# Transposes of half batch 12 and the first expert's weight rests moved behind the first list's one-hots; the logits of the last half batches in single groups

## The chip, the cores and the metric

The kernel runs on one core of a Trainium2 chip. The metric is the time of the whole program on the device, in microseconds (us), as the median of several executions. TensorE (PE) does the matrix products, VectorE (DVE) and ScalarE (ACT) the elementwise work, GpSimd (POOL) issues the indirect DMAs and did some subtractions, SyncE (SP) issues most other DMAs. Each engine works through its own queue strictly in the order in which the program was written for it, and waits there for results of others.

## The reference

```python
# 1. a causal 7-tap filter for each of 8 heads (weights: softmax over the taps)
out = np.einsum('hk,bskhg->bshg', w, x_unf)          # x: (8, 3584, 192)
# 2. a mixture of 8 experts with room for N/E = 3584 tokens each
x = out.reshape(28672, 192)
flat = (x @ w_gate).flatten()
for idx in np.argsort(-flat):                        # best (token, expert) pair first
    tok, e = idx // E, idx % E
    if assigned[tok] >= 0 or counts[e] >= cap: continue
    assigned[tok] = e; counts[e] += 1
for e in range(E):
    mask = assigned == e
    out[mask] = np.maximum(x[mask] @ w1[e], 0) @ w2[e]   # 192 -> 1024 -> 192
```

## The kernel before, in words

**Stages.** The 28672 tokens are 16 half batches of 1792. Stage one, up to some 160 us, runs over the half batches `i`: `load` brings `X`, `conv` makes eight products (`cv`, one for each head `h`), ACT copies each to the tile `a`, and a DMA stores `a` to `attn`. For the gate, DVE transposes `a` in four steps (`transp(i, u)`, tile `aT`), PE makes six groups of logits from it (`gates`, or `gate(i, u)` for two groups of it; into `pl`, copied to `L`), and `end(i)` transposes them (`pt`), copies them to `LT` (ACT) and takes the best logit of each token (`top`, DVE, tile `M1`). Stage two, the FFN, runs over 56 tiles of 512 tokens, expert by expert: POOL gathers the tokens (`xg`), PE transposes them, ACT and DVE split each number into a high and a low part (`xa`, `xd`), then for each of eight `f`: five products into `ph`, ACT takes the relu (`hh`), DVE the rest (`hl`), and PE multiplies with `w2` into `y`, one tile later.

**The lists.** Which tokens go to which expert is found in between. A first list needs only the first eight half batches: `sort` builds 16 one-hot tiles `oa` on DVE (`TENSOR_TENSOR oa<-irep,q`), PE multiplies with them (`bg<-X,oa`), ACT copies the sums; then `turn` (16 transposes `bg<-identb,X`, copied by ACT to `X`), `gather` (17 products, copied to `asm`) and `tokens` (16 small DVE operations that end in the index lists `ia`, `ja`). The first two tiles are gathered by `ja`; `todo` holds the transposes and splits of tile 0. A second and a third list follow during the FFN (`half(1)`, `rest`); there `sort4` sends its sums through DRAM (`otab`).

**What sets the order.** One Python program writes all queues. A conv step `(i, h)` calls `mid(h)` after its product and before ACT's copy of it; what `mid` writes there stands at that place in every engine's queue. The list steps are generators (`Steps`) that a hook advances when a model of the engines' times (`Pace`: `nc.pe`, `nc.dve`, `nc.act`) says that their inputs are ready. During tile 0 of the FFN the calls counted in `TAIL` advance the generator `tail` (the last logits). `wsplit` splits one piece of an expert's weights: ACT copies the high part (`w<-raw`), the engine given as an argument takes the rest (`w<-raw,w` or `dl<-raw,w`), and the raw buffer's next DMA is issued.

Where it stood before: from half batch 13 on (`LAG`), transposes and logits wait in the list `left` until the first list is written (`got`); the first four pieces of expert 0 are split at `(14, 1)`, `(14, 3)`, `(14, 5)` and `(14, 7)` with POOL as the engine; the logits of half batches 14 and 15 stand in `tail`.

Of the kernel before, what the change touches and what calls it, by code (L numbers as in the profile page):

```python
# [18 lines left out]
PEW, PEA = "pe", "pe after act"  # L19
# [9 lines left out]
class Meter:  # L29


    def __init__(self, pace, name, eng):
        self.pace, self.name, self.eng = pace, name, eng
# [226 lines left out]
class Route:  # L260
# [4 lines left out]
    def __init__(self, tc, nc, LT, cst, wk, drm):  # L265
        self.tc, self.nc, self.LT, self.cst, self.wk = tc, nc, LT, cst, wk
        self.cols = 0
        self.M1 = cst.tile([128, G], F32, name="M1")
        self.Ts = cst.tile([128, 1], F32, name="Ts")
        self.bad = cst.tile([128, 1], F32, name="bad")  # L270
        self.identr = cst.tile([128, 128], FR, name="ident")
        self.ident = self.identr.bitcast(F32)
        self.ltab = drm.tile([128, 8, G], F32, name="ltab")
        self.otab = [drm.tile([128, 16, 128], BF, name="otab%d" % q) for q in range(2)]
# [200 lines left out]
    def sort(self, h, nt, base, per=8):  # L475

        nc, wk = self.nc, self.wk
        V, A, PE = nc.vector, nc.scalar, nc.tensor
        O = self.O = wk.tile([128, 128, 16], BF, name="X1")
        q = []  # L480
        g0 = z = 0
        free = [0.0, 0.0]
        while z < 128:

            t = max(q[0][1] + nc.las, free[0] if z % 32 == 0 else 0.0) if q else 0.0
            if q and t <= nc.pe:
                if z == 64:
                    yield from self.columns(h, nt, base)
                a = q.pop(0)[0]
                if z % 32 == 0:  # L490
                    ps = self.bg()
                for u in range(per):
                    c = 16 * (z % 32 + u)
                    PE.matmul(ps[:, c:c + 16], a[:, :, u], self.b[:, :, :, z + u], start=True, stop=True,
                              skip_group_check=True)
                if z % 32 == 32 - per:
                    A.activation(O[:, z - 32 + per:z + per].rearrange("p g w -> p (g w)"), ps, AF.Copy)
                    free = [free[1], nc.act + nc.las]
                z += per
            elif g0 < 128 and len(q) < 5:  # L500
                a = self.oh_pool.tile([128, 128, per], BF, name="oa")
                V.tensor_tensor(a, self.irep[:, :, 0:per], self.q[:, None, g0:g0 + per].to_broadcast([128, 128, per]),
                                op=OP.is_equal)
                q.append((a, nc.dve))
                g0 += per
            else:

                yield t
                nc.pe = max(nc.pe, t)
                continue  # L510
            yield
        yield PEA
# [963 lines left out]
PERIOD, START = 8.8, 11.0  # L1476
LAG = 13

TAIL = (2, 3, 4, 7, 8, 9, 12, 13)


def moe_kernel(ctx, tc, x, weight, wg, w1, w2, out):
    nc = Pace(tc.nc)
    V, P = nc.vector, nc.gpsimd
# [4 lines left out]
    with ExitStack() as cw:  # L1489
# [8 lines left out]
        r = Route(tc, nc, LT, lst, wk, drm)  # L1498
        r.oh_pool = oh
        r.bg = lambda: bgp.tile([128, 512], F32, name="bg")  # L1500
        ff = FFN(tc, nc, attn, w1, w2, out, r.ident, wr, drm)
# [39 lines left out]

        def tail():

            for i in (14, 15):
                for u in range(3):
                    gate(i, u)
                    yield PEA if u == 2 else None
                end(i)
            nc.sync.dma_start(r.ltab, LT)
            c1.close()  # L1550
            cs.close()
            ff.wpool2(cw, 1)
            ff.hp[1] = pool(cw, "fh1", 1, **late)
            yield

        bg = Steps(nc, r, (half(0), tail(), half(1), rest()))
        bg.keep = 3
        cs, c1, ca, cl, cc = (ExitStack() for _ in range(5))
# [4 lines left out]
        k = build(cs, tc, nc, x, weight, wg, attn, LT, wk)  # L1563
# [15 lines left out]
        def end(i):  # L1579

            k.logits_t(i)
            r.top(i)

        def first():
            for e in range(2):
                ff.gather(e, [ja0[:, e, b:b + 1] for b in range(4)], NTOK // 2, P)


        todo = [partial(f, 0, *a) for u in range(2) for f, a in ((lambda i, u: ff.transp(i, u, r.bg()), (u,)), (ff.evac, (u,)))]
        got, left = [], []  # L1590

        def gate(i, u):
            for f in range(2 * u, 2 * u + 2):
                k.logits(i, f)

        def gates(i):
            for u in range(3):
                gate(i, u)

        def hook(at):  # L1600
            nc.pe = max(nc.pe, PERIOD * at / 8 + START)
            bg.hook(1.5)
            if not got and len(bg.gens) == 3:
                first()
                got.append(at)
            elif got and at >= got[0] + 10 and at % 8 in (2, 5) and todo:
                for _ in range(2):
                    todo.pop(0)()

        k.load(0)  # L1610
        k.toeplitz()
        k.gate_ops()
# [2 lines left out]
        for i in range(NHB):  # L1615
            if i + 3 < NHB:
                k.load(i + 3)
            if i == 4:
                r.consts_late()
            if i == 13:  # L1620
                cx[0].close()
                for _ in range(4):
                    ff.wload()
                ff.wpool(cw, 0, **late)

            def mid(h):

                if i and h == 0:
                    if i >= LAG:
                        left.append(partial(gates, i - 2))  # L1630
                    for u in range(4):
                        left.append(partial(k.transp, i - 1, u))
                        if 1 < i and (u == 3 or i < LAG):
                            left.append(partial(gate, i - 2, u) if u < 3 else partial(end, i - 2))
                for _ in range(2 if got else 1):
                    if left and (i < LAG or got):
                        left.pop(0)()
                if i >= 14 and h % 2:
                    ff.wsplit(-1, P)
                hook(8 * i + h)  # L1640

            k.conv(i, mid)
        for c in cx[1], cx[2], cx[3], cc:
            c.close()
        ff.pt = pool(cw, "pt", 1, space=PSUM, **right, **late)
# [3 lines left out]
        if not got:  # L1649
            first()  # L1650
        bg.keep = 0
        for f in left + todo:
            f()
        for u in range(4):
            k.transp(15, u)
# [25 lines left out]
        def steps():  # L1681
            if len(bg.gens) == 3:
                calls.append(0)
                if len(calls) in TAIL:
                    bg.run()
# [45 lines left out]
```

## Time and profile before

| what | value |
|---|---|
| median of 3 runs (lowest, highest) | 1240.46 us (1240.14, 1240.78) |
| the profiled execution, its own time | 1242.93 us |
| its span, first to last instruction | 1241.2 us |
| TensorE busy | 1202.9 us, 97% of the span |
| VectorE busy | 983.0 us, 79% |
| ScalarE, GpSimd busy | 565.0 and 537.8 us |
[...]

The profiled execution is 2.47 us longer than the median. The page shows TensorE busy in all but a few places, so what counts is where it is not: the waits of PE, and the chain of work that leads to each. Nearly all instructions carry line 56, the helper that records them, so operations are told apart by their tiles. A row of the chain shows only the time that the piece adds to the chain; a row in order of time shows the instruction's own duration, which overlaps its neighbours on a pipelined engine.

### The profile page before, as it was taken

What the parts mean: (1) busy time and instruction counts of PE and PEld (TensorE: products, weight loads), DVE (VectorE), ACT (ScalarE), POOL (GpSimd) and SP (SyncE); (2) the same over time, 40 slices, a digit from 0 to 9 for tenths busy, and PEclk for the clock granted to TensorE, in tenths of its full rate; (3) what the DMA queues carried; (4) which work ended last, traced back from release to release, by engine and by line L of the source; (5) the groups of instructions that cost most, each with busy time, mean ns of one, the idle gap of its engine ahead of it and who ended that gap; (6) DMA issues with size and microseconds to landing.
All of it is one profiled execution on the core that took longest, in us unless ns stands there. A gap on an engine that the chain in (4) does not pass through costs nothing.

```text
span 1241.2 us, 21781 instructions
## 1 busy us (share of the span) xinstructions
PE 1202.9 (97%) x7694; PEld 1036.0 (83%) x7694; DVE 983.0 (79%) x2117; ACT 565.0 (46%) x1252; POOL 537.8 (43%) x528
## 2 busy tenths in 40 slices
PE   4899999999999999999999999999999999999997
PEld 2445678899989989889888889999999999999997
DVE  7389689898998989989979865777777777777772
ACT  4454565556445455454554433343333333343332
POOL 3000254435556555555455435434534444543522
PEclk9999999999999999999999999999999999999999
DMA  9999774658527474756344342114223222413100
GB/s 212 331 348 320 234 244 120 155 170 287 174 76 213 135 241 124 223 158 193 89 131 120 108 106 73 41 41 158 90 104 105 100 98 96 155 64 131 48 23 29
DMA packets 129221, 182.03 MB, mean 147 GB/s; under 512 B 21632, under 2 KB 91728, under 8 KB 127440
## 3 DMA queue, kind: packets, MB, share of 16 engines
q1 hardware_dynamic: 86496, 104.15, 27.5%
q0 software_dynamic: 21504, 44.07, 11.9%
q10 hardware_dynamic: 21104, 32.34, 7.9%
q8 instruction: 62, 1.02, 0.4%
q14 instruction: 55, 0.45, 0.1%
HBM read 102.38 MB, written 78.12 MB: 145 GB/s over the span
## 4 chain that ended last, share of the span: by engine, by line
PE 89%; DVE 4%; DMA 4%; ACT 1%; issue 1%; SPq 0%; POOL 0%; ACTq 0%; POOLq 0%; DVEq 0%
PE ph L56 42%; PE y L56 40%; PE bg L56 3%; PE cv L56 3%; DMA X<-in_x_dram 2%; DVE aT L56 1%; DVE X L56 1%; PE pl L56 1%; DMA wgr<-in_moe_w_gate_dram 1%; PE px L56 0%; DMA otab<-X 0%; SPq L189 0%; DMA X<-otab 0%; ACT a L56 0%; ACT X L56 0%
## 5 line engine op out<-in xcount | busy, mean ns | idle before, releaser
L56 PE MATMUL y<-w,hh 128*128 128x384 f32 x1792 | 536.4, 355 | 0.0
L56 ACT ACTIVATE hh<-ph 128x512 fp32r<-128x512 f32 x448 | 267.6, 598 | 477.6 <-PE ph L56 472.3
L56 PE MATMUL y<-w,hl 128*128 128x192 f32 x1792 | 449.7, 251 | 0.0
L56 DVE SCALAR_TENSOR_TENSOR hl<-ph,hh 128x512 fp32r<-128x512 f32 x448 | 308.1, 688 | 137.6 <-ACT hh L56 133.1
L56 PE MATMUL ph<-xa,w 128*128 128x512 f32 x1344 | 395.7, 402 | 0.0
L56 PEld LDWEIGHTS y<-w,hl 128*128 128x128 f32 x1792 | 341.6, 191 | 16.3
L56 PEld LDWEIGHTS y<-w,hh 128*128 128x128 f32 x1792 | 336.9, 188 | 19.7 <-issue 1.7
L1367 POOL DMA_INDIRECT out_dram<-yo,ia x128 | 145.1, 1134 | 216.5 <-DVE yo L56 184.7
L56 PEld LDWEIGHTS ph<-xa,w 128*128 128x128 f32 x1344 | 219.0, 189 | 20.2 <-issue 1.2
L1367 POOL DMA_INDIRECT out_dram<-yo,ib x96 | 95.9, 999 | 220.1 <-DVE yo L56 212.8
L56 PE MATMUL ph<-xd,w 128*128 128x512 f32 x448 | 178.0, 397 | 1.2 <-DVE xd L56 1.2
L56 PE MATMUL ph<-xd,dl 128*128 128x512 f32 x448 | 174.4, 389 | 0.3 <-DVE dl L56 0.3
L56 DVE STREAM_TRANSPOSE xs<-xg 32x128 f32<-32x128 f32 (+2 forms) x408 | 164.8, 404 | 6.6
L1292 POOL DMA_INDIRECT xg<-attn,ja x128 | 140.6, 1098 | 46.4 <-issue 40.7
L56 PE MATMUL cv<-X,TH 118*128 118x384 f32 x256 | 99.9, 518 | 21.3 <-DMA X<-in_x_dram 12.4
L56 ACT ACTIVATE yt<-y 128x192 f32<-128x192 f32 x224 | 73.0, 326 | 94.6 <-PE y L56 92.1
L1292 POOL DMA_INDIRECT xg<-attn,jb x96 | 103.4, 1077 | 29.3 <-issue 29.3
L56 DVE TENSOR_TENSOR yo<-y,yt 128x192 f32<-128x192 f32 x224 | 79.3, 354 | 38.4 <-ACT yt L56 35.9
L56 PEld LDWEIGHTS ph<-xd,w 128*128 128x128 f32 x448 | 84.3, 188 | 21.5 <-DVE xd L56 1.7
L56 PEld LDWEIGHTS ph<-xd,dl 128*128 128x128 f32 x448 | 84.4, 188 | 19.9 <-issue 0.5
L56 PEld LDWEIGHTS cv<-X,TH 118*128 118x128 f32 x256 | 45.2, 196 | 52.0 <-issue 14.1
L56 ACT ACTIVATE a<-cv 128x384 f32<-128x384 f32 x128 | 59.2, 493 | 50.7 <-PE cv L56 33.3
(238 smaller groups left out, 916.0 us busy)
## 6 DMA issues: line engine op xcount, KB each, us to landing
attn<-a ACTq DMA_DIRECT2D x16, 1344.0 KB, 11.9
X<-in_x_dram SPq DMA_DIRECT2D x17, 672.0 KB, 12.3
raw<-in_moe_w_dram SPq DMA_DIRECT2D x56, 192.0 KB, 3.1
X<-in_x_dram ACTq DMA_DIRECT2D x15, 672.0 KB
kw<-w SPq DMA_DIRECT2D x36, 256.0 KB, 3.4
kv<-w SPq DMA_DIRECT2D x24, 384.0 KB, 4.4
scr<-xs SPq DMA_DIRECT2D x96, 96.0 KB, 2.5
w<-kw SPq DMA_DIRECT2D x6, 1536.0 KB
```

The costliest lines, as they stand in the source:

```text
L56: return f(*a, **k)
L1292: self.nc.gpsimd.indirect_dma_start(out=t[:, b], out_offset=None, in_=self.attn[0:rows], in_offset=bass.IndirectOffsetOnAxis(ap=idx[b], ax ...
L1367: st = self.nc.gpsimd.indirect_dma_start(out=self.out, out_offset=bass.IndirectOffsetOnAxis(ap=idx, axis=0), in_=o, in_offset=None, bounds ...
```

## The change

`Route.sort` now sets `made` once all 16 one-hots are written. From the next conv step on, `mid` writes two entries of the new list `more` at each step: a transpose of half batch 12 and one piece of expert 0's weights, with DVE instead of POOL as the engine of the subtraction, and with `nc.dve` set back afterwards, so that the model does not see them. The table `last` writes out what stood in `left`: transposes of half batches 13 and 14 at `(14, 4..7)` and `(15, 2..5)`; all six logit groups of 11, 12 and 13 in one go at `(13, 6)`, `(14, 2)`, `(15, 1)`, each followed by its `end` one step later; the steps of `todo` at `(15, 4)` and `(15, 6)`. The logits of 14 now stand behind the last conv, before the FFN; `tail` keeps only 15, at other calls (`TAIL`). The number of operations is the same, apart from the engine of four subtractions.

```diff
--- before.py
+++ after.py
@@ -265,6 +265,7 @@
     def __init__(self, tc, nc, LT, cst, wk, drm):
         self.tc, self.nc, self.LT, self.cst, self.wk = tc, nc, LT, cst, wk
         self.cols = 0
+        self.made = False
         self.M1 = cst.tile([128, G], F32, name="M1")
         self.Ts = cst.tile([128, 1], F32, name="Ts")
         self.bad = cst.tile([128, 1], F32, name="bad")
@@ -503,6 +504,7 @@
                                 op=OP.is_equal)
                 q.append((a, nc.dve))
                 g0 += per
+                self.made = g0 == 128
             else:
 
                 yield t
@@ -1476,7 +1478,7 @@
 PERIOD, START = 8.8, 11.0
 LAG = 13
 
-TAIL = (2, 3, 4, 7, 8, 9, 12, 13)
+TAIL = (6, 7, 8, 11, 12)
 
 
 def moe_kernel(ctx, tc, x, weight, wg, w1, w2, out):
@@ -1541,11 +1543,10 @@
 
         def tail():
 
-            for i in (14, 15):
-                for u in range(3):
-                    gate(i, u)
-                    yield PEA if u == 2 else None
-                end(i)
+            for u in range(3):
+                gate(15, u)
+                yield PEA if u == 2 else None
+            end(15)
             nc.sync.dma_start(r.ltab, LT)
             c1.close()
             cs.close()
@@ -1603,10 +1604,20 @@
             if not got and len(bg.gens) == 3:
                 first()
                 got.append(at)
-            elif got and at >= got[0] + 10 and at % 8 in (2, 5) and todo:
-                for _ in range(2):
-                    todo.pop(0)()
-
+
+        split = partial(ff.wsplit, -1, V)
+        more = [partial(k.transp, 12, 0), split, partial(k.transp, 12, 1), split, partial(k.transp, 12, 2), split,
+                partial(k.transp, 12, 3), split]
+        last = {}
+        for i, h in ((14, 4), (15, 2)):
+            for u in range(4):
+                last[i, h + u] = [partial(k.transp, i - 1, u)]
+        for i, h in ((13, 6), (14, 2), (15, 1)):
+            last.setdefault((i, h), []).append(partial(gates, i - 2))
+            last.setdefault((i, h + 1), []).append(partial(end, i - 2))
+        for h in (4, 6):
+            last.setdefault((15, h), []).extend(todo[h - 4:h - 2])
+        del todo[:]
         k.load(0)
         k.toeplitz()
         k.gate_ops()
@@ -1625,21 +1636,26 @@
 
             def mid(h):
 
-                if i and h == 0:
-                    if i >= LAG:
-                        left.append(partial(gates, i - 2))
+                if r.made:
+                    d = nc.dve
+                    for _ in range(2):
+                        if more:
+                            more.pop(0)()
+                    nc.dve = d
+                for f in last.get((i, h), ()):
+                    f()
+                if i and h == 0 and i < LAG:
                     for u in range(4):
                         left.append(partial(k.transp, i - 1, u))
-                        if 1 < i and (u == 3 or i < LAG):
+                        if i > 1:
                             left.append(partial(gate, i - 2, u) if u < 3 else partial(end, i - 2))
-                for _ in range(2 if got else 1):
-                    if left and (i < LAG or got):
-                        left.pop(0)()
-                if i >= 14 and h % 2:
-                    ff.wsplit(-1, P)
+                if left:
+                    left.pop(0)()
                 hook(8 * i + h)
 
             k.conv(i, mid)
+        gates(14)
+        end(14)
         for c in cx[1], cx[2], cx[3], cc:
             c.close()
         ff.pt = pool(cw, "pt", 1, space=PSUM, **right, **late)
@@ -1649,7 +1665,7 @@
         if not got:
             first()
         bg.keep = 0
-        for f in left + todo:
+        for f in left:
             f()
         for u in range(4):
             k.transp(15, u)
```

On DVE, behind the last four one-hots (`oa`) of the first list and ahead of the first operation of `tokens` (`m_f<-asm`); `aT<-a` are the transposes of half batch 12, `w` and `dl` the low parts of expert 0, `M` the best logits of half batch 11:

```order
+L56 STREAM_TRANSPOSE aT<-a 128x768
+L56 TENSOR_TENSOR w_1430<-raw,w_1430 128x512
+L56 STREAM_TRANSPOSE aT<-a 128x768
+L56 TENSOR_TENSOR dl<-raw,w_1430 64x512
+L56 STREAM_TRANSPOSE aT<-a 128x768
+L56 TENSOR_TENSOR w_1430<-raw,w_1430 128x512
+L56 STREAM_TRANSPOSE aT<-a 128x768
+L56 TENSOR_TENSOR dl<-raw,w_1430 64x512
+L56 TENSOR_REDUCE M_76<-LT 128x16
 L56 TENSOR_SCALAR m_f<-asm 128x32
```

These nine rows stood later: four transposes behind `tokens`, the `M` behind them, and the subtractions on POOL, ahead of the gathers of tiles 0 and 1.

On PE, the end of the conv and the start of tile 0, before (`ident,xg` transposes tile 0's tokens, `cv` is a conv product, `ph` the first layer, `aT,c_mu` logits, `px` the transposes of tile 1):

```order
L56 MATMUL bg<-ident,xg 128x128 x4
L56 MATMUL cv<-X,TH 128x384 x2
L56 MATMUL bg<-ident,xg 64x128 x4
L56 MATMUL ph<-xa,w_1548 128x512 x3
L56 MATMUL ph<-xd,w_1548 128x512
L56 MATMUL ph<-xd,dl 128x512
L56 MATMUL bg<-aT,c_mu 32x128 x16
L56 MATMUL ph<-xa,w_1548 128x512 x3
L56 MATMUL bg<-aT,c_mu 32x128 x8
L56 MATMUL ph<-xd,w_1548 128x512
```

and now:

```order
L56 MATMUL bg<-ident,xg 128x128 x4
L56 MATMUL cv<-X,TH 128x384 x2
L56 MATMUL bg<-ident,xg 64x128 x4
L56 MATMUL cv<-X,TH 128x384
L56 MATMUL pl<-aT,c_mu 32x128 x24
L56 MATMUL pt<-ident,L 128x128
L56 MATMUL ph<-xa,w_1430 128x512 x3
L56 MATMUL ph<-xd,w_1430 128x512
L56 MATMUL ph<-xd,dl 128x512
L56 MATMUL ph<-xa,w_1430 128x512 x3
L56 MATMUL ph<-xd,w_1430 128x512
L56 MATMUL ph<-xd,dl 128x512
```

The transposes of tile 0 stand one conv step earlier, the logits of half batch 14 (`pl`, 24 rows) ahead of the first `ph` rather than between the first ones.

On DVE, from the end of `tokens` to the first rests of tile 0 (`hl`), before:

```order
L56 TENSOR_SCALAR ja_112<-m_y 128x32
L56 STREAM_TRANSPOSE aT<-a 128x768 x4
L56 TENSOR_REDUCE M_76<-LT 128x16
L56 STREAM_TRANSPOSE aT<-a 128x768 x4
L56 TENSOR_REDUCE M_76<-LT 128x16
L56 STREAM_TRANSPOSE aT<-a 128x768 x4
L56 TENSOR_REDUCE M_76<-LT 128x16
L56 TENSOR_TENSOR xa<-bg,xa 128x512
L56 TENSOR_TENSOR xd<-bg,xd 64x512
L56 STREAM_TRANSPOSE aT<-a 128x768 x4
L56 SCALAR_TENSOR_TENSOR hl<-ph,hh 128x512
```

and now:

```order
L56 TENSOR_SCALAR ja_112<-m_y 128x32
L56 TENSOR_REDUCE M_76<-LT 128x16
L56 STREAM_TRANSPOSE aT<-a 128x768 x5
L56 TENSOR_REDUCE M_76<-LT 128x16
L56 STREAM_TRANSPOSE aT<-a 128x768 x2
L56 TENSOR_TENSOR xa<-bg,xa 128x512
L56 STREAM_TRANSPOSE aT<-a 128x768
L56 TENSOR_TENSOR xd<-bg,xd 64x512
L56 TENSOR_REDUCE M_76<-LT 128x16
L56 STREAM_TRANSPOSE aT<-a 128x768 x4
L56 SCALAR_TENSOR_TENSOR hl<-ph,hh 128x512
```

Eight transposes of half batches 13 and 14 are left where there were twelve of 12, 13 and 14, and the `M` of half batch 14 now stands ahead of the four transposes of 15, where it stood behind the second `hl`. On ACT the copies `w<-raw` of the four pieces now stand between the conv copies ahead of `turn`'s, and in the second list's `sort4` and `gather` PE's rows are displaced by one `ph` or `y` block.

## Rows read from the trace of the kernel before

**Rows 1.** PE's waits from 128 to 182 us: us in total, times, longest.

```profile
PE pl L56 <- DVE aT L56: 1.7, 4, 0.5
PE ph L56 <- DVE xd L56: 1.2, 1, 1.2
```

**Rows 2.** The chain that ended last, 128 to 182 us: start, us, what.

```profile
135.49 2.03 PE cv L56 x6
137.53 0.51 PE bg L56 x8
...
138.06 1.87 ACT X L56 x2
...
141.54 0.39 ACT asm L56
...
146.56 0.18 DVE ja L56
146.75 3.47 DVE aT L56 x4
...
154.01 1.48 PE pl L56 x48
...
157.73 0.45 PE bg L56 x4
...
177.03 0.47 PE ph L56
177.50 1.12 PE y L56 x8
```

**Rows 3.** DMA queue 1 (SP's), 138 to 139 us: packets, MB, share of 16 engines.

```profile
q1 hardware_dynamic: 4, 0.00, 1.2%
```

**Rows 4.** DVE in order of time: start, us, operation [idle before <-releaser].

```profile
141.95 0.18 DVE L56 TENSOR_SCALAR m_f<-asm 128x32 f32<-128x32 f32 x1 [8.29 <-ACT asm L56]
...
143.02 1.26 DVE L56 TENSOR_SCALAR m_i<-m_f,off 128x32 int32<-128x32 f32 x1
144.32 1.22 DVE L56 SCALAR_TENSOR_TENSOR m_y<-m_i,m_y 128x32 f32<-128x32 int32 x1
...
161.79 3.56 DVE L56 STREAM_TRANSPOSE aT<-a 128x768 f32<-128x768 f32 x4
165.27 0.65 DVE L56 SCALAR_TENSOR_TENSOR hl<-ph,hh 128x512 fp32r<-128x512 f32 x1
...
176.20 0.69 DVE L56 TENSOR_TENSOR dl<-raw,w 64x512 fp32r<-64x512 f32 x1
```

**Rows 5.** POOL in order of time, the same columns.

```profile
142.96 1.28 POOL L1268 TENSOR_TENSOR w<-raw,w 128x512 fp32r<-128x512 f32 x1 [32.52 <-ACT w L56]
144.21 1.27 POOL L1268 TENSOR_TENSOR dl<-raw,w 64x512 fp32r<-64x512 f32 x1
...
147.65 1.25 POOL L1292 DMA_INDIRECT xg<-attn,ja  x1 [1.50 <-issue]
...
151.82 1.00 POOL L1292 DMA_INDIRECT xg<-attn,ja  x1 [0.31 <-issue]
```

**Rows 6.** Tile `xg`, 140 to 185 us: from issue to landing.

```profile
DMA to landing us min/median/max: 2.7/3.5/5.2
```

**Rows 7.** Groups by shape, 128 to 182 us: xcount | busy us, mean ns.

```profile
L56 DVE TENSOR_REDUCE M<-LT 128x16 f32<-128x128 f32 x6 | 2.1, 354 | 0.3 <-ACT LT L56 0.3
L56 DVE TENSOR_TENSOR w<-raw,w 128x512 fp32r<-128x512 f32 x2 | 1.4, 678 | 0.0
```

**Rows 8.** DVE's waits from 128 to 182 us.

```profile
DVE hl L56 <- ACT hh L56: 1.6, 2, 1.0
```

**Rows 9.** PE's waits over the whole span.

```profile
PE bg L56 <- DMA X<-otab: 2.4, 1, 2.4
```

**Rows 10.** By stretch: PE, PEld, DVE, ACT, POOL busy (x); granted clock; DMA; GB/s.

```profile
200.00:220.00 20.00, 20.00 (x142) 17.82 (x142) 19.59 (x37) 11.41 (x25) 9.32 (x8) 1.00 0.49 137
...
740.00:760.00 20.00, 20.00 (x107) 18.10 (x108) 10.78 (x30) 7.03 (x14) 8.79 (x9) 0.93 0.27 75
```

## Prediction

> **What bounds the kernel now.** I read the page first: TensorE is busy in 97% of the span, so only its waits can be won, and from 182 us to the end the chain of waits is nearly all PE. Next come PE's waits by stretch. In the handover from the conv to the FFN, 128 to 182 us, PE waits 1.7 us for transposes `aT` and 1.2 us for `xd` of tile 0 [rows 1]. The chain in order of time shows why [rows 2]: behind the first list's one-hots come the copies of `turn` on ACT, `asm`, the sixteen operations of `tokens` up to `ja`, then four transposes of half batch 12 that PE needs, all one behind the other. DVE meanwhile sat idle for 8.29 us until `asm` [rows 4]. Last I read DVE in order of time: from 165.27 us, the first `hl`, to 176.89 us, the end of the first `dl` of the next expert (176.20 + 0.69), it sets the pace [rows 4], with only 1.6 us of waiting [rows 8]. PE's first `y` product at 177.50 us follows that `dl` by one `ph` product of 0.47 us [rows 2]. From there on PE is full, so I count when that first `y` comes.
>
> **The change part by part.** No queue differs up to the last one-hot products, so the count starts at 135.49 us, where they end [rows 2].
>
> *Into the gap, on DVE.* Four transposes (3.47 us for four [rows 2]) and four subtractions (0.68 us each on DVE [rows 7], 1.28 on POOL [rows 5]) take 6.2 us of the 8.29 idle. They need ACT's four high parts, and those the raw weights. SP's queue moves its last four packets between 138 and 139 us [rows 3]; no row dates each piece, but the last is there by 139. Its copy comes up on ACT at about 138.5, so it waits 0 to 0.5 us, ahead of the copy of the logits of half batch 11, which is not due before 139.7. I take nothing; beyond 139.7 every microsecond would pass on to the list.
>
> *The list comes later.* PE now does four convs (2.03 / 3 = 0.68 each [rows 2]) and the 24 logit rows of half batch 11 (1.48 [rows 2]) ahead of `turn`, before it was three convs: 135.49 + 2.71 + 1.48 = 139.68. Eight transposes (0.51) and ACT's two copies (1.87) end at 142.06; before they ended at 138.06 + 1.87 = 139.93. From there to `asm` took 1.61 us (141.54 - 139.93); one small copy to `LT` is added, put at 0.2, so `asm` starts at 143.87, and `tokens` 0.41 later (141.95 - 141.54) at 144.28, 2.3 us later than before.
>
> *But `tokens` is shorter.* It took 4.79 us, 141.95 to 146.74 [rows 2, 4]. The first nine operations, all on 128x32, took 1.07 us (to 143.02), the last seven 3.72. The two longest, `m_i` and `m_y`, run to 144.28 and 145.54; POOL's subtractions run to 144.24 and 145.48 [rows 4, 5]. The small operations end where POOL's end, as if they were held. Those POOL instructions are gone. At the pace of the first nine the rest takes 0.8 to 1.2 us: 2.1 in all, so `ja` is ready at 146.4 (before 146.74). The bound above is the old 4.79, that below is none, since no row of this kind is shorter.
>
> [...]
>
> *Gathers and the conv's end.* POOL issues 0.91 us after `ja` (147.65 - 146.74), the fourth gather 4.17 later [rows 5]: 151.5. Landing takes 2.7 to 5.2 us, 3.5 in the median [rows 6]: 154.2 to 155.0, with 154.5 taken, since little else is under way. On PE: the other half of `turn`, three convs, a transpose and the 17 list products (0.55, the same as before) end at 143.4; eight convs, the logits of 12 and a transpose 7.0, to 150.4. The transposes of 13 on DVE end at 146.4 + 0.35 [rows 7] + 3.47 = 150.2, so the old wait of 1.7 us is gone. Logits of 13 and three convs 3.6, to 154.0; waiting for tokens 0.5; transposes of tile 0 (0.45 twice [rows 2]) and three convs, to 157.4; logits of 14, to 158.9.
>
> *What is late next.* The best logits `M` of half batch 14 now stand on DVE ahead of the four transposes of 15. They need those logits, a copy, a transpose, a copy and `M`'s own 0.35, by estimate 1.0 together: 159.9. Then the transposes, 3.48 (165.27 - 161.79 [rows 4]): the first `hl` at 163.4, 1.9 us earlier than before. PE gives two `ph` by then and waits about 1.4 us for the logits of 15; that wait is new, and hidden, since DVE sets the pace.
>
> *The stretch on DVE.* It took 11.62 us. One `M` (0.35) is gone from it. Of the 1.6 us of waiting [rows 8] between none and all stays; I take 0.5, nearer to none, because two `hh` lie ready and PE has only one half batch of logits left to put between its `ph`, not two. 163.4 + 11.62 - 0.35 - 1.1 = 173.6, against 176.89: **3.3 us earlier**, and the first `y` with it. TAIL and the removed branch in `mid` move steps between neighbours only; cost nothing, under the same DVE pace.
>
> **The sum.** The profiled execution took 1242.93 us, 2.47 more than the median. Minus 3.3 is 1239.6 for a profiled one, 1237.2 us for the median. Landing (0.3 better, 0.5 worse), waits on DVE (0.5 better, 1.1 worse) and small steps make the likeliest case 1236.0 to 1238.6.
>
> **The rivals.**
>
> *`tokens` stays at 4.79 us.* Everything from `ja` on comes 2.7 later and PE has no slack there: 1239.9. For it: `m_i` and `m_y` turn numbers into integers or read them. Against: the same ends on POOL. Chance 0.08.
>
> *Part is given back in the FFN.* From 200 to 220 us DVE is busy 19.59 of 20 us [rows 10], and list steps are displaced there by a block; `hl` could come late and hold `ph`. For it: that row. Against: PE had no wait there, and DVE's work does not grow. At half the gain: 1238.8. Chance 0.12.
>
> *Slower: the second list's detour through DRAM comes into the open.* Between its last one-hot products and PE's `gather` there is now one `y` block less, 1.12 us [rows 2]. [...] Against: PE had no wait at this place, so some slack was there. Chance 0.08, half of it beyond 0.2%.
>
> That the change does not do what it says is excluded by the order of the queues.
>
> **How the numbers follow.** Likeliest case 0.70, `tokens` 0.08, given back 0.12, second list 0.08, better than 1236.0 0.02. The range 1235.9 to 1240.0 leaves out the second list, the best, and a little of the rest. A measurement of this kernel tells some 0.2%, 2.5 us, from no change: faster is below 1238.0. That is five sixths of the likeliest case and the best, 0.60; slower 0.04, rounded up to 0.05 for the third list, which has a wait already; the same 0.35.
>
> **What would show it.** Right: DVE's idle time ahead of `m_f` falls from 8.29 to some 4 us in two pieces; `m_i` and `m_y` under 0.3 us each; `ja` near 146.5; the first `hl` near 163.4 and the first `y` near 174.2; no wait of PE for `aT` of 12, one of about 1.4 us for that of 15. Wrong: a wait of ACT for the raw weights, `ja` after 148, a new wait of PE at the second list's `gather`, or `hl` held in the first tiles.

## The result, and the profile after

| what | before | after |
|---|---|---|
| median of 12 runs each, taken side by side | 1240.89 us | 1244.72 us |
| ratio of after to before, 95% interval | | 1.0029 [1.0021, 1.0037] |
| the profiled execution, its own time (span) | 1242.93 (1241.2) us | 1246.24 (1244.2) us |
| first one-hots' end to the first `y` | 42.00 us | 46.54 us |
| of that PE busy, idle | 38.84, 3.16 us | 40.99, 5.55 us |
| TensorE's granted clock in that stretch | 1.00 | 0.96 |

The change made the kernel 0.29% slower, 3.6 us of 1240.9 by the ratio (3.8 between the medians); 1237.2 us was forecast, with a chance of 0.05 for slower. The span grew by 3.0 us, and the first `y` product comes 3.07 us later, so all of it lies ahead of that `y`. From there to the end it is 1063.8 us in both.

The start of a program varies a little: in this execution the last one-hot products end 1.5 us earlier than in that of before. So I count from the start of the convs right behind them (135.34 before, 133.87 after), and call the stretch from there to the first `y` the **handover**. These are its rows of the two kernels, before and then after. The columns are the stretch, the busy time (and number of instructions) of PE, PEld, DVE, ACT and POOL, the granted clock, DMA share and GB/s:

```profile
135.34:177.34 42.00, 38.84 (x385) 25.70 (x383) 31.17 (x56) 26.81 (x64) 23.57 (x23) 1.00 0.68 224
```

```profile
133.87:180.41 46.54, 40.99 (x385) 26.30 (x383) 29.58 (x58) 26.72 (x63) 17.90 (x18) 0.96 0.61 201
```

PE does the same 385 pieces of work. Its idle time grew by 2.39 us (5.55 - 3.16), and its busy time by 2.15 us (40.99 - 38.84), at a granted clock of 0.96 against 1.00. The two make the 4.54 us of the handover, of which the earlier start hides 1.5.

PE's waits from 128 to 182 us after the change, which answer to [rows 1] (total, times, longest):

```profile
PE bg L56 <- DMA xg<-attn,ja: 3.5, 1, 3.5
PE pt L56 <- ACT L L56: 0.8, 2, 0.6
PE bg L56 <- DVE aT L56: 0.8, 2, 0.5
```

Both old waits are gone, the 1.7 us for `aT` and the 1.2 us for `xd`. One new wait is longer than the two together: PE stands still for the gathered tokens of tile 0. PE in order of time shows where, and what it does to the work behind it (start, us, operation, in brackets the idle time ahead and what ended it):

```profile
152.49 1.45 PE L56 MATMUL cv<-X,TH 118*128 118x384 f32 x4
153.78 0.27 PE L56 MATMUL bg<-ident,xg 128*128 128x128 f32 x1
157.59 0.69 PE L56 MATMUL bg<-ident,xg 128*128 128x128 f32 x3 [3.54 <-DMA xg<-attn,ja]
158.12 2.02 PE L56 MATMUL cv<-X,TH 118*128 118x384 f32 x4
159.94 1.06 PE L56 MATMUL bg<-ident,xg 128*64 128x128 f32 x4
160.79 1.49 PE L56 MATMUL cv<-X,TH 118*128 118x384 f32 x2
162.21 1.54 PE L56 MATMUL pl<-aT,c_mu 128*32 128x128 f32 x48
```

Four `cv` products take 2.02 us behind the wait and 1.45 ahead of it. The rows by stretch say why:

```profile
153.70:158.00 4.30, 0.76 (x5) 0.32 (x3) 1.41 (x2) 0.12 (x1) 3.38 (x4) 1.00 0.49 155
158.00:162.00 4.00, 4.00 (x12) 2.00 (x11) 1.92 (x3) 2.33 (x5) 1.61 (x3) 0.61 0.12 34
```

PE is busy for 0.76 of 4.3 us, and in the 4 us behind that the granted clock is 0.61: 0.94 from 158 to 159 us, and 0.50 in each of the three us from 159 to 162.

The chain that ended last names the transfer (start, us, what). Here it replaces [rows 2]:

```profile
119.48 13.91 DMA attn<-a
133.40 5.34 DMA raw<-in_moe_w_dram
138.82 0.63 ACT w L56
...
146.22 0.19 DVE ja L56
...
148.86 8.69 DMA xg<-attn,ja
157.59 0.69 PE bg L56 x3
...
162.28 1.52 PE pl L56 x48
```

The second gather of tile 0 was issued at 148.86 and landed 8.69 us later. Tile `xg`, 140 to 160 us, from issue to landing, before and then after (answers to [rows 6], which also holds a later tile). The view knows the landing of only two of tile 0's four gathers in each kernel: the first and the third before, the second and the third after.

```profile
DMA to landing us min/median/max: 2.7/2.8/2.9
```

```profile
DMA to landing us min/median/max: 7.6/8.1/8.7
```

What stood in the way is ACT's store of half batch 14. It was issued at 153.16 before, behind tile 0's four gathers, and now at the very time of the second; counted from the start of the handover that is 14.99 us instead of 17.82. ACT's queue, before and then after:

```profile
153.16 0.31 ACTq L205 DMA_DIRECT2D attn<-a  x1
```

```profile
148.86 0.31 ACTq L205 DMA_DIRECT2D attn<-a  x1
```

The DMA queues from 150 to 153 us (packets, MB, share of 16 engines), before and then after; q0 is POOL's, q10 is ACT's:

```profile
q0 software_dynamic: 121, 0.22, 24.8%
```

```profile
q10 hardware_dynamic: 316, 0.97, 100.1%
```

Before, the gathers had the engines to themselves. After, not one packet of a gather moves in these 3 us, while the store fills all sixteen engines. Only three gathers are held: by the trace's records of landings, sixteen for each gather with some missing, the first (issued at 147.30) was in by 150.06, undisturbed. PE transposed its tokens at 153.78 without a wait.

The store is not the whole wait. Of the second gather fifteen of the sixteen parts had landed at 155.00, and the last at 157.55; the third and the fourth show the same (155.24 and 157.73, 155.46 and 157.91). So some 2.5 of PE's 3.54 us were spent on one late part. Between the two times the trace has, behind the last packets of the store, one packet of 16 KB on the queue for instructions, busy from 155.52 to 156.47. The queues from 155 to 156 us:

```profile
q8 instruction: 1, 0.02, 5.9%
```

The runs below with the raw piece late, tile 0 late and `M` late show it too: two or three of the last three gathers have one part 2.1 to 2.4 us behind the fifteen others, and such a packet ahead of it. No run moves that packet alone, so its share in the delay is not shown.

Earlier in the chain stands another wait that the forecast put at 0 to 0.5 us, ACT's for the last raw piece of the first expert's weights:

```profile
138.82 0.63 ACT L56 ACTIVATE w<-raw 128x512 fp32r<-128x512 f32 x1 [1.99 <-DMA raw<-in_moe_w_dram]
```

### The profile page after: what moved, and what is told of

Its sections match the earlier page's. It is cut to its first block, busy times and chain, and to the rows that moved or that the text cites. A ratio compares the mean times of both kernels' runs of the same rounds, so it can differ in the third digit from the quotient of the medians.

```text
span 1244.2 us, 21777 instructions
## 1 busy us (share of the span) xinstructions
PE 1206.4 (97%) x7694; PEld 1037.0 (83%) x7694; DVE 982.6 (79%) x2121; ACT 566.5 (46%) x1252; POOL 533.3 (43%) x524
## 4 chain that ended last, share of the span: by engine, by line
PE 88%; DMA 5%; DVE 4%; issue 1%; ACT 1%; SPq 1%; POOL 0%; POOLq 0%; ACTq 0%; DVEq 0%
PE ph L56 42%; PE y L56 40%; PE bg L56 3%; PE cv L56 2%; DMA X<-in_x_dram 1%; DVE aT L56 1%; DMA attn<-a 1%; DVE X L56 1%; DMA wgr<-in_moe_w_gate_dram 1%; PE pl L56 1%; DMA xg<-attn,ja 1%; PE px L56 0%; DMA raw<-in_moe_w_dram 0%; DMA otab<-X 0%; DMA X<-otab 0%
```

## The experiments

Four theories. **T1**: the store, now earlier, holds the gathers back. **T2**: ACT's wait for the last raw piece makes the list late. **T3**: on DVE, `M` of half batch 14 holds the transposes of 15. **T4**: the landing is late, but costs PE time only because convs and logits are queued behind tile 0's transposes. Ratios are to runs of the kernel before made beside each kernel, with 95% intervals. For the four experiments that come first these had a median of 1241.39 us. The others ran on two other chips, where the kernel before itself took 1247.41 us (the next three) and 1246.70 us (the last two), so only ratios are compared across groups. A handover is that of one traced execution. Its start alone lies between 131.99 and 135.34 us in the traces of the kernel before, the change and these four, and no trace of the kernel before was taken on the other two chips; the last five handovers are not to be compared with its 42.00.

| kernel | ratio to before | median, before beside it | handover |
|---|---|---|---|
| the change | 1.0029 [1.0021, 1.0037] | 1244.72, 1240.89 | 46.54 |
| store of 14 late | 0.9992 [0.9982, 1.0001] | 1240.44, 1241.39 | 40.40 |
| last raw piece late | 1.0015 [1.0004, 1.0025] | 1243.22, 1241.39 | 46.88 |
| tile 0 behind the logits of 14 | 0.9987 [0.9978, 0.9995] | 1239.03, 1241.39 | 40.77 |
| `M` of 14 behind transposes of 15 | 1.0012 [1.0002, 1.0022] | 1242.76, 1241.39 | 44.59 |
| store late, a second store in its place | 1.0027 [1.0009, 1.0046] | 1250.88, 1247.41 | 50.22 |
| tile 0 late, transposes of 15 ahead of it | 0.9984 [0.9971, 0.9997] | 1246.45, 1247.41 | 41.54 |
| only the idle stretch filled | 1.0023 [1.0008, 1.0037] | 1250.20, 1247.41 | 49.31 |
| the same, last raw piece late | 0.9995 [0.9986, 1.0005] | 1246.70, 1246.70 | 45.10 |
| tile 0 late and last raw piece late | 0.9991 [0.9981, 1.0001] | 1246.26, 1246.70 | 42.02 |

**The store later.**

```diff
-        A.dma_start(attn[i * 1792:(i + 1) * 1792]..., a[0:W]...)
+        k.store = lambda: A.dma_start(attn[i * 1792:(i + 1) * 1792]..., a[0:W]...)
+        if i != 14:
+            k.store()
...
+        last.setdefault((15, 4), []).insert(0, lambda: k.store())
```

> The changed kernel with one edit: the store of half batch 14 (1344 KB) is issued at conv step (15, 4), ahead of the transposes of tile 0, and no longer right behind conv 14. Theory T1 (the store, issued 4.3 us earlier than before the change, locks tile 0's gathers out of the DMA engines; PE then waits 3.5 us and the granted clock falls): the gathers land some 3 us after their issue, PE waits under 1 us for xg, the granted clock stays at 1.00 behind it, the first y comes 4 to 5 us sooner; 1240 to 1241 us against 1244.7. Theory T2 (the list is late because ACT waits 2.0 us for the last raw piece): PE still waits about 3 us for xg; 1244 to 1245.

It moved the time by 0.37% (1.0029 to 0.9992), and the handover by 6.1 us. The landing of tile `xg`, 140 to 160 us (here two of tile 0's gathers, 2.9 and 4.0 us, and one of a later tile), and PE at the same place:

```profile
DMA to landing us min/median/max: 2.9/3.6/4.0
```

```profile
151.35 0.67 PE L56 MATMUL bg<-ident,xg 128*128 128x128 f32 x4
153.16 0.60 PE L56 MATMUL bg<-ident,xg 128*64 128x128 f32 x4
```

There is no wait, and the granted clock is 1.00 in every stretch of 5 us from 140 to 180. T1 stands: where the store does not meet the gathers of tile 0, the wait and the loss are gone. The store now meets the gathers of the second tile instead, for which PE waits 1.6 us at 160.97.

**The store later, and the traffic put back.**

```diff
         if i != 14:
             k.store()
+        else:
+            k.again()
+        k.again = k.store
```

> The kernel of the run with the late store (store of half batch 14 at (15, 4)), and at the place where that store had stood, behind conv 14, the store of half batch 13 once more: the same 1344 KB to the same rows as before, which nobody waits for. T1 (it is the traffic that holds the gathers back): PE waits 3 to 4 us for xg again, the granted clock falls behind it; 1244 to 1246 us. If the order of half batch 14's own rows mattered, or the late issue itself helped: as the run with the late store, 1240 to 1241.

Adding the same bytes back takes the ratio from 0.9992 to 1.0027. From 151 to 154 us the queues show the picture of the change, again without a packet of q0, and in order of time PE waits for tile 0 twice:

```profile
q10 hardware_dynamic: 306, 0.94, 99.6%
```

```profile
156.73 0.33 PE L56 MATMUL bg<-ident,xg 128*128 128x128 f32 x1 [0.98 <-DMA xg<-attn,ja]
158.34 0.58 PE L56 MATMUL bg<-ident,xg 128*128 128x128 f32 x2 [1.28 <-DMA xg<-attn,ja]
```

That is 2.3 us, less than the 3 to 4 expected, since PE came 1.3 us later, counted from the start of the handover (21.21 against 19.91). The granted clock behind it is 0.73 from 160 to 165 us. The added store has a side effect too: ACT's copy of the logits of 14 waits 4.4 us for something that the profile does not name ("remote"), which belongs to no theory here. So the run shows that the traffic is enough to hold the gathers back; its whole time is no measure of that alone.

**The raw piece later.**

```diff
-                partial(k.transp, 12, 3), split]
+                partial(k.transp, 12, 3)]
...
+        last.setdefault((14, 6), []).append(split)
```

> The changed kernel with one edit: the fourth piece of expert 0's weights is split at (14, 6), no longer ahead of the copies of turn, so ACT does not wait for its raw data there. T1: the list ends some 1.3 to 2 us earlier, but so does conv 14 with its store, and the gathers still meet it; PE's wait for xg shrinks by 1 us at most: 1243.5 to 1245. T2: the whole delay goes, PE's wait for xg with it: 1241 to 1242.5.

The first gather is issued 12.26 us from the start of the handover (144.25), after the change 13.43 (147.30). Little of that 1.2 us is the edit's, for the runs with the store late, tile 0 late and `M` late, which leave the piece where it was, have 12.24, 12.79 and 12.66. The store is issued 14.31 us from the start (146.30), after the change 14.99, and PE still waits:

```profile
152.71 0.33 PE L56 MATMUL bg<-ident,xg 128*128 128x128 f32 x1 [0.87 <-DMA xg<-attn,ja]
156.19 0.50 PE L56 MATMUL bg<-ident,xg 128*128 128x128 f32 x2 [3.15 <-DMA xg<-attn,ja]
```

The handover is as long as before this edit (46.88 us), but the traced execution, 1246.19 us, is the slowest of the twelve. The median, 1243.22 us, lies between the two forecasts (T1 from 1243.5, T2 to 1242.5), and the two intervals overlap. So T2 is not the whole cause: the wait for `xg` stays, and the time stays above that of the kernel before. A share of some 0.1% for it is neither shown nor excluded. That the wait is not harmless shows below.

**Tile 0 behind the logits of 14.**

```diff
-        for h in (4, 6):
-            last.setdefault((15, h), []).extend(todo[h - 4:h - 2])
-        del todo[:]
...
         gates(14)
+        for f in todo:
+            f()
         end(14)
```

> The changed kernel with one edit: the transposes and splits of tile 0 stand behind the logits of half batch 14 and no longer at (15, 4) and (15, 6). Theory T4 (the landing is late, but it costs only because PE's last convs and the logits of 14 are queued behind it): PE does 3.6 us of convs and logits meanwhile, waits under 0.5 us for xg, the granted clock stays at 1.00; first y about 5 us sooner, 1239.5 to 1241. If instead what is late is behind it (M of 14, transposes of 15 on DVE), half of that: 1242 to 1243.

This is the largest gain of the four: 0.42% against the change, and 0.13% faster than the kernel before. The store is still early (146.80, the same time as the second gather), but PE has three conv steps and the logits in hand meanwhile. The eight transposes follow with no wait that the view shows, just in time, for by the trace's records the second gather is complete at 155.68:

```profile
153.75 1.73 PE L56 MATMUL pl<-aT,c_mu 128*32 128x128 f32 x48
155.41 1.44 PE L56 MATMUL bg<-ident,xg 128*128 128x128 f32 x8
```

T4 stands beside T1: the loss needs both the late landing and the place of tile 0's transposes in PE's queue. Taking away either one undoes it.

**`M` of half batch 14 later.**

```diff
-        end(14)
+        k.logits_t(14)
...
             k.transp(15, u)
+        r.top(14)
```

> The changed kernel with one edit: the best logits M of half batch 14 are taken on DVE behind the four transposes of half batch 15, not ahead of them. Theory T3 (M, which waits for the logits of 14, holds the transposes of 15 and with them the first hl): the transposes begin with the last copy of a at 162.8 and not at 165.28, the first hl comes 2.2 us earlier, about 166.5: 1242 to 1243. T1 alone (the logits of 14 are late, the transposes would wait for a anyway): at most 0.4 us, 1244.3 or more.

The transposes of 15 on DVE, after the change and then here:

```profile
165.28 3.55 DVE L56 STREAM_TRANSPOSE aT<-a 128x768 f32<-128x768 f32 x4
```

```profile
162.58 3.56 DVE L56 STREAM_TRANSPOSE aT<-a 128x768 f32<-128x768 f32 x4 [0.42 <-ACT a L56]
```

PE's wait for `xg` is no shorter (3.9 us), and still the handover is 1.95 us shorter. So T3 is right in its mechanism: a late `M` passes PE's delay on to DVE, 2 of the 4.5 us. It is no cause of its own, for with the wait for `xg` gone it no longer decides, as far as the next kernel tells.

**Tile 0 late, and the transposes of 15 ahead of it.**

```diff
         gates(14)
+        for u in range(4):
+            k.transp(15, u)
         for f in todo:
             f()
         end(14)
...
-        for u in range(4):
-            k.transp(15, u)
```

> The kernel of the run with the transposes of tile 0 behind the logits of 14 (1239.0 us), and the four transposes of half batch 15 ahead of them on DVE, so that they wait neither for tile 0's gathers nor for M of 14. T3 (DVE's order still sets the first hl): they run from 154 to 157.5 in place of 158.8 to 162.3, the first hl comes 2 us earlier, and the first y 1 to 1.5 us, since PE has some 1.5 us of waits left there: 1237.5 to 1238.2. If PE itself sets the pace by now: 1239.0, within 0.4 us.

The ratio, 0.9984, is within the error of 0.9987. DVE is done with the transposes at 159.54, and the first `hl` comes at 162.33; it waits for its `ph`, which waits for `xa`. So DVE's order no longer sets the pace, as far as the intervals tell. Both kernels beat the one before, by an interval that just excludes no change.

**Only the idle stretch filled**, in the kernel before.

```diff
...
+        split = partial(ff.wsplit, -1, V)
+        more = [f for u in range(4) for f in (partial(k.transp, 12, u), split)]
...
+                if r.made:
+                    d = nc.dve
+                    for _ in range(2):
+                        if more:
+                            more.pop(0)()
+                    nc.dve = d
...
-                        left.append(partial(k.transp, i - 1, u))
+                        if i != 13:
+                            left.append(partial(k.transp, i - 1, u))
...
-                if i >= 14 and h % 2:
-                    ff.wsplit(-1, P)
```

> The kernel before the change with one part of it: the four transposes of half batch 12 and the first four pieces of expert 0's weights stand on DVE behind the first list's one-hots; logits, TAIL, tile 0 and all else keep their old order. T1 (the filling itself gains, and the store of 14 that then comes early spoils it only where it meets the gathers of tile 0): tokens takes 2.2 us, the store of 14 is issued behind conv 14 some 2 to 3 us earlier than before, late enough to miss the first gathers or not needed by PE that early; 1238.5 to 1240. T2 (the filling holds up the list, since ACT waits for the last raw piece): the list comes no sooner and nothing is gained; 1241 to 1242.5.

Alone, the filling is 0.23% slower. Here it is T2: `tokens` takes 2.25 us, but the list starts late. PE and the granted clock:

```profile
139.90 0.91 PE L56 MATMUL cv<-X,TH 118*128 118x384 f32 x2 [0.46 <-ACT a L56]
142.11 2.86 PE L56 MATMUL cv<-X,TH 118*128 118x384 f32 x4 [1.30 <-ACT a L56]
```

```profile
140.00:145.00 5.00, 3.70 (x8) 1.63 (x9) 0.18 (x1) 3.77 (x7) 0.00 (x0) 0.72 0.52 154
```

ACT waits 1.59 us for the last raw piece. The copies of the conv's products stand behind it, PE runs out of free product banks twice and stops, and four `cv` take 2.86 us at a granted clock of 0.72. In the change the 48 logit products of half batch 11 stand there and need no bank of the conv's; PE has no wait there in the change, though ACT waits longer (1.99 us). So by the traces the order of the logits, which the forecast counted only as 1.48 us of delay to the list, is what made the filling bearable; no run moves these logits alone.

**The same, and the last raw piece later.** The fourth `split` moves to `(14, 6)`, as above.

> The kernel with only the idle stretch filled (0.23% slower than before the change), with one more edit: the fourth piece of expert 0's weights is split at (14, 6), not ahead of the copies of turn. T2 (ACT's wait for the last raw piece holds the copies of a behind it, PE runs out of product banks twice, 1.8 us in all, the granted clock falls to 0.72 of the upper level and the list is late): none of this remains, ja comes 3 us earlier, the time falls by 3 to 5 us: 0.997 to 1.000 of before. If the filling costs for another reason (fewer transposes behind the list, so that PE waits elsewhere): within 1 us of 1.0023.

From 1.0023 to 0.9995: the 0.28% are that one wait and what stands behind it. `ja` starts 9.79 us from the start of the handover (142.37), against 13.86 (148.14). What is left of the idea of filling the stretch is no measurable gain.

**Tile 0 late and the raw piece late.** The two edits above together.

> The changed kernel with the transposes of tile 0 behind the logits of half batch 14 and the fourth piece of expert 0's weights split at (14, 6): the two edits together. T4 (with tile 0 behind the logits PE has work throughout, about 1.3 us of waits are left up to 165 us, and an earlier list brings little): 0.9980 to 0.9990 of before, no better than the first edit alone (0.9987). T2 (the wait for the raw piece delays PE's own work): another 1.5 us, 0.9970 to 0.9978.

The ratio is 0.9991, no better than tile 0 late alone. The list is little earlier, though: the first gather is issued 12.26 us from the start of the handover, 12.79 with tile 0 late alone. Where PE is covered, these 0.5 us bring nothing that the intervals show.

## Why the prediction was wrong, point by point

The forecast's own times and the measured ones, both counted from the start of the handover (135.34 and 133.87), in us:

| step | forecast | measured | later by |
|---|---|---|---|
| `ja` ready | 11.06 | 12.53 | 1.47 |
| first gather issued | 11.96 | 13.43 | 1.47 |
| PE at tile 0's transposes | 18.66 | 19.91 | 1.25 |
| its wait for `xg` | 0.5 | 3.54 | 3.04 more |
| logits of 14 begin | 22.06 | 28.34 | 6.28 |
| first `hl` | 28.06 | 34.88 | 6.82 |
| first `y` | 38.86 | 46.54 | 7.68 |

**The failed step is the landing.** The forecast took the last gather's landing at 154.5, 3 us from its issue, "since little else is under way". The second and the third gather took 8.7 and 7.6 us, the last 6.5 by the trace's records, and PE waited 3.5 us, not 0.5. The forecast gave the gathers a time near that of free engines, and forgot that its own edits bring the conv forward, and with it the store at its end. I counted the DMAs of what the diff moves by name, not those of what comes earlier by itself. The late sixteenth part, which makes up some 2.5 us of the wait, was in no term either.

Why the gathers moved nothing beside the store is not shown. By the trace's records the store moves as 448 packets of 3 KB, by estimate 28 for each of the 16 engines (448 / 16), and from 150 to 153 us q10 stands at 100.1%, without a packet of q0; whether the gathers' packets were queued by then no row tells. What was measured is the time to landing: 8.7 and 7.6 us.

**What the delay cost behind the landing.** Behind PE's 3.54 us of waiting the granted clock was lower, 0.61 over 4 us, and the handover's work took about 2 us more (busy time 40.99 against 38.84). The late logits of 14 held `M` and with it the transposes of 15. I had `M` there, as a step that takes 0.35 us and not as a link that passes on a delay. From the first `hl` to the first `y` the forecast took off 1.4 us; it was 0.4 (11.66 us against 12.07).

**The bound that I did not check.** Even without the store, 3.3 us was not to be had. From the first one-hots' end to the first `y` PE has 38.84 us of work in the row of before, in a stretch of 42.00: 3.16 us is all that it stands idle there. The forecast took 3.3 and at the same time allowed PE two new waits, 0.5 and 1.4 us, calling the second hidden "since DVE sets the pace". With these it could claim 1.3 us at most (3.16 - 1.9). The runs without the collision show about that: 0.9992 and 0.9987 of the time of before, 1.0 and 1.6 us, and in the traces a handover shorter by 1.6 us (store late) and 1.2 us (tile 0 late).

**The raw weights.** "I take nothing" was wrong: 1.99 us. SP's last piece was issued at 133.40, behind the landing of a store of `attn`, and landed 5.34 us later, at a time of its own that does not move with the sort: up to there the change and the runs with the store late, tile 0 late and `M` late are the same kernel, and ACT waits 1.99, 0.79, 1.33 and 1.21 us in their traces. What it cost the time of the change is not shown; in the kernel that has the filling alone it was the whole loss. The forecast named this wait among what would make it wrong, and priced it by what it does to the list, not by the copies that stand behind it on ACT.

**Right.** `tokens`: from 144.15 to 146.40, 2.25 us, where 2.1 were forecast and 4.79 were measured before. DVE in order of time, answering to [rows 4]:

```profile
144.15 0.18 DVE L56 TENSOR_SCALAR m_f<-asm 128x32 f32<-128x32 f32 x1 [1.23 <-ACT asm L56]
...
145.22 0.23 DVE L56 TENSOR_SCALAR m_i<-m_f,off 128x32 int32<-128x32 f32 x1
...
145.49 0.19 DVE L56 SCALAR_TENSOR_TENSOR m_y<-m_i,m_y 128x32 f32<-128x32 int32 x1
```

`m_i` fell from 1.26 to 0.23 us and `m_y` from 1.22 to 0.19, with POOL idle (busy for 0.00 of the 2.25 us). So these operations are not slow by themselves. That POOL's subtractions held them was an estimate from their common ends; how the one could hold the other is not shown. The rival that `tokens` stays at 4.79 us is out, and DVE's wait ahead of `m_f` did shrink, to 5.5 us in four pieces where some 4 in two were forecast.

Out as well are the other two rivals. Nothing was given back in the FFN (1063.8 us from the first `y` to the end in both), and from 200 to 220 us PE is as full as in [rows 10]. At the second list PE has no new wait, so what one would cost there no run shows; the one for the third list's `otab` is 2.2 us (2.4 in [rows 9]). The slower side came by a mechanism that was none of the rivals: a transfer that moved itself.

## What to carry to other kernels

When an edit lets a stage end earlier, list what that stage issues at its end, its stores above all, and look whom they now meet: a landing time read where the engines were free holds only while they stay free (2.7 to 2.9 us here, 6.5 to 8.7 beside the store). Before believing a gain, take the busy time of the engine that bounds the stretch from the row of before; what it stands idle there is the most that any reordering can win. And where a queue waits for a transfer, put work that does not need it ahead of the wait, as the run with tile 0 behind the logits of 14 does.

## What was not expected of the hardware

- One 1344 KB store on ACT's queue kept three gathers of POOL's queue from moving anything for 3 us (150 to 153 us, 316 packets to none); they landed after 6.5 to 8.7 us, before the change after 2.7 to 2.9.
- The last of a gather's sixteen parts landed some 2.5 us behind the fifteen others, behind a 16 KB packet for instructions. With the store late there is such a packet too, at 148.87, away from any store; there the third gather's last part came 1.3 us behind the rest (151.42 against 150.09).
- The trace of the kernel before already held the lesson. The 5.2 in [rows 6] belongs to four gathers that were issued from 162.78 to 166.71, behind the store of half batch 15, issued at 160.02. The view leaves out tile 1's gathers, issued from 153.84 to 157.75 behind the store of half batch 14: by the trace's records they landed after 4.6 to 7.8 us, and from 156 to 157 us, before the change, the queues show the store and no packet of q0:

```profile
q10 hardware_dynamic: 109, 0.33, 99.7%
```

- A wait of 3.54 us of PE was followed by a granted clock of 0.61 over 4 us. In the kernel with the filling alone two shorter waits of PE, 0.46 and 1.30 us, end at 139.90 and 142.11, and the granted clock from 140 to 145 us is 0.72.
